# RWKV-7 attention fused with a cosine-gated feed-forward block: one scaling moved to VectorE, a product tree cut in three and moved, one step taken forward, three small products moved apart

## The chip, the cores and the metric

The kernel runs on one core of one Trainium2 chip. The metric is device time in microseconds (us) of one execution; the median of 3 runs of the kernel before is 802.15 us (800.43 to 803.71). The engines are named as in the profile: PE is TensorE's matmul, PEld its weight load, DVE VectorE, ACT ScalarE, POOL GpSimd, SP the engine whose queue issues nearly all DMAs here.

## The reference

For each of 4 batches and 8 heads a 40 x 40 state is carried over 768 tokens; the result feeds a feed-forward block with 2048 hidden units, whose weights arrive as float64.

```python
y[:, :, t] = einsum('bhd,bhde->bhe', rt, state)
Sa = einsum('bhde,bhe->bhd', state, at)
state = state * wt[:, :, None, :] - einsum('bhd,bhe->bhde', Sa, bt) \
        + einsum('bhd,bhe->bhde', vt, kt)
...
x = y.transpose(0, 2, 1, 3).reshape(B * S, H * D)   # 3072 x 320
h = x @ w_in                                        # 320 x 2048
out = (h * cos(h)) @ w_out                          # 2048 x 320
```

## The kernel before

The recurrence is done in chunks of C = 32 tokens, 24 chunks in all, all batches and heads at once. A chunk c has five steps in its chain, which `main(c)` returns (L922): t (`ch_t`, L650: transposes of the state qz into s), q (`ch_q`, L661: qps from s and rT), x (`ch_x`, L676: x0ps from the triangle ag, vvm, aT and qz; copied out by ACT L696 and DVE L697), s (`ch_s`, L700: sps from the inverse rt and x0; DVE L719 makes sm), z (`ch_z`, L726: dps from kn, vvm, bn and sm; DVE L755 and L762 read it, POOL L756 scales the state by the chunk's decay, and L767 scales the output tile yt by wx). Two steps after z, `tokens` (L772) writes yt to a DRAM tile xd, and one step later reads it back transposed as xT, all in SP's queue, which runs in order.

Beside the chain, `p2(c+1)` (L914) prepares the next chunk in steps v, k and g: transposes (L605, L614) and the Gram matrices `gram` (L619), which DVE L637, ACT L642 and DVE L643 copy out. `p1(c)` prepares two chunks' decays and the triangular systems (pw, pa, pb, pn). The inverse rt of four chunks' systems is built at DVE; for chunks 0 to 7 it is done in two blocks, and the off-diagonal block is made on PE: `pair_first` (F1 to F7, L546) and `pair_second` (S1 to S7, L560), each 64 small matmuls into a tile `below`, S ending with an addition into rt on DVE (L567). Chunk n's step s needs Sn.

The running products of the decays of chunks 4 to 23 are taken for four chunks at once: `ws_fetch(q)` (L159, 640 KB) loads them, `ws_scan(q)` (L166) multiplies them in nine DVE instructions, five up a tree (L170) and four down (L175), and `ws_store(q)` (L178) writes them to DRAM, from where `load` reads them. q = 2 stands for chunks 8 to 11.

The feed-forward block is cut in pieces over pairs of chunks: `first_a` and `first_b` (the hidden layer `ph`, 256 tokens by 512 units), then two `second` (into `po`). `first_b` computes the 64-row tail of w_in first if the step before it was marked `small` (L820), else last. Weights are turned from float64 to float32 in the first 140 us by `rounded` (L224): per tile a DMA `words`, DVE L245, L246, L255, L261, ACT L249, L251, L258 and POOL L264. These go into a list `w_steps`.

The order is written out by hand. For every chunk there is a list `segs` of steps, with M where a piece goes. `step` (L346) issues a step's instructions, then whatever `later(n, ...)` had put n steps ahead, then some instructions off the lists of the inverse and of the weights: in chunk 2 two of `w_steps` per step (none after an F or S), in chunk 3 two and three. Engines run what they are issued in order, so this list is the order of every engine. `FILL` (L1049) puts idle bf16 matmuls into PE's stream ahead of some places; `busy` (L955) puts idle 128x512 ones after a step:

```python
step(seg, *((0, 0) if c < 3 and seg in (*firsts, *seconds) else fill), small=seg in (...))
if seg not in (*firsts, *seconds) and (c < 2 or c == 2 and not done):
    busy({s: 6, q: 5, v: 4, k: 4, z: 4}.get(seg, 3))
```

`done` counts the pieces issued so far; it is 0 until chunk 2's first M. PSUM tiles named `at` (L324: sT, vT, qps, kT, x0ps, gram, sps, below, dps, wT, aps, bT, nps) share a ring of two buffers, so each waits until the tile two before it has been read.

Of the kernel before, what the change touches and what calls it, by code (L numbers as in the profile page):

```python
# [12 lines left out]
ALU = mybir.AluOpType  # L13
# [7 lines left out]
def kernel(  # L21
# [43 lines left out]
    nc = tc.nc  # L65
    B, H, S, D = r.shape
    P, C, DP = 128, 32, 64
# [95 lines left out]
            bass.AP(w.tensor, w.offset + q * n, [[S * D, B * H], [C * D, 4], [1, C * D]]),  # L163
        )

    def ws_scan(q):  # L166
        n = 1
        while n < C:
            to = ws[:, 2 * n - 1 :: 2 * n]
            nc.vector.tensor_tensor(to, to, ws[:, n - 1 :: 2 * n], ALU.mult)  # L170
            n *= 2
        n = C // 4
        while n:
            to = ws[:, 3 * n - 1 :: 2 * n]
            nc.vector.tensor_tensor(to, to, ws[:, 2 * n - 1 : C - 1 : 2 * n], ALU.mult)  # L175
            n //= 2

    def ws_store(q):  # L178
        wd[q] = dram.tile([B, H, 4, C, D], F32, tag="wd", name="wd")
# [166 lines left out]
    def step(work, of_inv=0, of_w=0, small=False):  # L346


        before = list(waiting)
        work()  # L350
        G["small"] = small and G["kind"]
        for w in before:
            w[0] -= 1
            if w[0] == 0:
                waiting.remove(w)
                w[1]()
        for steps, n in ((inv_steps, of_inv), (w_steps, of_w)):
            for _ in range(min(n, len(steps))):
                steps.pop(0)()
# [366 lines left out]
    def ch_z(c):  # L726
        ps = [at("dps") for _ in range(2)]
        sm = G["sm"]

        wide = c > 3  # L730
        for bb in range(0 if wide else B):
            for e in range(2):
                mm(
                    ps[bb // 2][full[e], bb % 2, : 4 * N72], idle[blk[bb], :DP],
                    pick(idle[blk[bb]], 0, (0, 4), (1, N72)), True,
                )
        for s, n in ((0, kn_b[c % 2]), (1, bn_b[c % 7])):
            for j in range(4):
                o = C - C * (j // 2)
                for bb in range(B):  # L740
                    for e in range(2):
                        first = wide and not s
                        mm(
                            ps[bb // 2][(full if first else half)[e], bb % 2, j * N72 : (j + 1) * N72],
                            n[blk[bb], 2 * j + e, : DP if first else D],
                            sm[e][blk[bb], j, :] if s else vvm[c % 2][blk[bb], 2 * j + e, o : o + N72],
                            first and j == 0,
                        )
        wx, wc = G["wx", c], G["wc", c]
        yt = sb1.tile([P, 4, B, C], F32, tag="yt", name="yt")  # L750
        for bb in range(B):
            dp = ps[bb // 2][:, bb % 2]
            if c < NCH - 1:
                z = pick(qz[:, bb], C, (DP, 2), (NZ, 2), (1, D))
                nc.vector.tensor_tensor(z, pick(dp, 0, (2 * N72 + C, 2), (N72, 2), (1, D)), z, ALU.add)  # L755
                nc.gpsimd.tensor_tensor(  # L756
                    z, z,
                    wc.rearrange("p (f m b) -> p f m b", f=2, m=2)[:, :, :, bb]
                    .unsqueeze(3).to_broadcast([P, 2, 2, D]),
                    ALU.mult,  # L760
                )
            nc.vector.tensor_tensor(  # L762
                yt.rearrange("p (f m) b t -> p f m b t", f=2)[:, :, :, bb],
                pick(dp, D, (2 * N72 - D, 2), (N72, 2), (1, C)),
                pick(qz[:, bb], 0, (NZ - C, 2), (NZ, 2), (1, C)), ALU.add,
            )
        nc.gpsimd.tensor_tensor(  # L767
            yt.rearrange("p j b t -> p (j b) t"), yt.rearrange("p j b t -> p (j b) t"), wx, ALU.mult
        )
        later(2, lambda: tokens(c, yt))  # L770
# [133 lines left out]

        return [first_w, both_a, lambda: p1_b(c), lambda: p1_n(c)]

    def scanned(q):

        ws_scan(q)
        later(2, lambda: ws_store(q))  # L910
        if q + 1 < NCH // 4:
            later(12, lambda: ws_fetch(q + 1))
# [17 lines left out]
    with tc.manual_schedule():  # L930
# [71 lines left out]
        v, k, g = p2(0)  # L1002
# [43 lines left out]
        firsts = [lambda n=n: pair_first(0, n, n > 2) for n in range(4)]  # L1046
        seconds = [lambda n=n: pair_second(0, n, n > 2) for n in range(4)]
        (F1, F2, F3), (S1, S2, S3) = firsts[1:], seconds[1:]
        FILL = {(1, 6): 6, (1, 9): 14, (2, 0): 6, (2, 3): 6, (2, 5): 4, (2, 11): 29, (3, 3): 13, (3, 4): 20}  # L1049
        for c in range(NCH):  # L1050
            t, q, x, s, z = main(c)
            v, k, g = p2(c + 1) if c + 1 < NCH else [lambda: None] * 3
# [2 lines left out]
            if c == 0:  # L1055
                segs = []
            elif c == 1:
                segs, fill = [t, F1, v, q, k, S1, x, g, s, z], (1, 4)
            elif c == 2:
                for n, m, name in ((11, 5, "a"), (14, 4, "b")):  # L1060
                    later(n, lambda m=m, name=name: load(m, name))
                segs, fill = [t, F2, v, q, S2, k, M, x, M, F3, g, M, s, S3, M, z, M, M], (0, 2)
            elif c == 3:
                pw4, pa4, pb4, pn4 = p1(4)
                pw, pa, pb, pn = p1(6)
                segs = [
                    t, pw4, M, q, pa4, M, x, lambda: scanned(2), M, s, pw, M, pb4, pa, M, pn4, M, z, M,
                    pb, v, pn, k, M, g,
                ]
                for n, m, name in ((1, 5, "b"),):  # L1070
                    later(n, lambda m=m, name=name: load(m, name))
                fill = (2, 3)
            elif c == 4:
                pw, pa, *p8 = p1(8)
                firsts = [lambda n=n: pair_first(4, n) for n in range(4)]
                seconds = [lambda n=n: pair_second(4, n) for n in range(4)]
                F4, F5, F6, F7 = firsts
                S4, S5, S6, S7 = seconds
                segs = [
                    t, v, M, q, M, k, x, M, F4, M, S4, F5, M, s, F6, M, pw, F7, M, z, M, g, M, pa, S5, lambda: scanned(3),  # L1080
                ]
                fill = (2, 0)
            elif c == 5:
                pw, pa = p1(10)[:2]
                pb, pn = p8
                segs = [t, M, pb, q, M, pn, k, M, x, M, s, S6, M, z, M, S7, M, pw, v, M, g, pa, M]
            elif c % 4 == 0 and q0 < NCH:
                pb, pn = p1(q0)[2:]
                segs = [t, v, M, q, M, k, x, M, g, M, s, pb, M, z, M, pn, M, M]
                if q0 + 4 < NCH:  # L1090
                    segs.insert(-1, lambda: scanned(c // 4 + 2))
            elif c % 4 == 1 and q0 < NCH:
                pw, pa = p1(q0 + 2)[:2]
                segs = [t, M, pw, q, M, x, k, M, s, v, M, z, M, pa, M, g, M, M]
            elif c % 4 == 2 and q0 < NCH:
                pb, pn = p1(q0 + 2)[2:]
                segs = [t, M, pb, q, M, pn, v, M, x, M, s, k, M, g, M, z, M, M]
            elif c % 4 == 3 and q0 + 4 < NCH:
                pw, pa = p1(q0 + 4)[:2]
                segs = [t, M, pw, q, M, x, k, M, s, v, M, z, M, pa, M, g, M, M]  # L1100
            else:
                segs = [t, v, M, q, M, x, k, M, g, M, s, M, M, z, M, M]
# [10 lines left out]
            for i, seg in enumerate(segs):  # L1113
                kept_busy(FILL.get((c, i), 0))
                while seg is s and ("rt", c) not in G:
                    if allowed(c):
                        piece(4, 0)
                    else:
                        inv_steps.pop(0)()
                while seg is pn4 and w_steps:  # L1120
                    w_steps.pop(0)()
                if seg is not M:
                    G["kind"] = "q" if seg is q and c > 3 else "other"
                    step(seg, *((0, 0) if c < 3 and seg in (*firsts, *seconds) else fill), small=seg in (q, x, g, s, z, pn, pn4, *firsts, *seconds))
                    if seg not in (*firsts, *seconds) and (c < 2 or c == 2 and not done):
                        busy({s: 6, q: 5, v: 4, k: 4, z: 4}.get(seg, 3))
                else:
                    place += 1
                    if place * empty // places > (place - 1) * empty // places:
                        continue  # L1130
                    if allowed(c) and (c != 4 or done < 23):
                        piece(*fill)
                while i == n - 1 and c > 3 and done < goal and c != 4 and allowed(c):
                    piece(*fill)
                if seg is pn and (c == 3 or c > 4 and c % 4 == 2):
                    inv_steps.extend(by_blocks(q0) if c == 3 else inverse(q0))
# [36 lines left out]
```

## Time and profile before

| what | value |
|---|---|
| median of 3 runs | 802.15 us (800.43 to 803.71) |
| the profiled execution: its own time | 800.58 us |
| its span (first to last instruction) | 798.9 us |
| PE busy in the span | 745.9 us (93%) |
| PE busy, 0 to 100 us | 68.98 of 100 us |
| PE busy, 100 to 260 us | 148.65 of 160 us |
| PE busy, 260 to 740 us | 474.96 of 480 us |
| DVE busy, 60 to 100 us / 100 to 120 / 120 to 160 | 36.06 of 40 / 11.70 of 20 / 33.59 of 40 us |

The profile is one execution, taken by the hardware profiler. Its first lines give each engine's busy time. Its timeline gives, per group of like instructions, the start, the length from the first start to the last end, the engine, the line, what is written and read, the shape, the count, and in brackets the engine's idle time just before it with what ended that. "issue" there means that the engine waited for nothing that the profile shows. The view by windows gives busy time and number of instructions of each engine in a stretch, and then the clock that TensorE was granted there as a share of full speed, the DMA engines' busy share and GB/s. Chunk 2 runs from about 93 to 129 us, chunk 3 to 170, chunk 4 to 206, chunk 5 to 242.

### The profile page before, as it was taken

What the parts mean: (1) busy time and instruction counts of PE and PEld (TensorE: products, weight loads), DVE (VectorE), ACT (ScalarE), POOL (GpSimd) and SP (SyncE); (2) the same over time, 40 slices, a digit from 0 to 9 for tenths busy, and PEclk for the clock granted to TensorE, in tenths of its full rate; (3) what the DMA queues carried; (4) which work ended last, traced back from release to release, by engine and by line L of the source; (5) the groups of instructions that cost most, each with busy time, mean ns of one, the idle gap of its engine ahead of it and who ended that gap; (6) DMA issues with size and microseconds to landing.
All of it is one profiled execution on the core that took longest, in us unless ns stands there. A gap on an engine that the chain in (4) does not pass through costs nothing.

```text
span 798.9 us, 39602 instructions
## 1 busy us (share of the span) xinstructions
PE 745.9 (93%) x17812; PEld 571.0 (71%) x17812; DVE 486.7 (61%) x1025; ACT 383.4 (48%) x723; POOL 199.9 (25%) x354
## 2 busy tenths in 40 slices
PE   4768798999999999999999999999999999999997
PEld 4535576777766777777777787777787777777775
DVE  8768858864734896554895645994346863323331
ACT  1336567564435436545535635534545445354352
POOL 5326635230321330330330230332031122201000
PEclk9888899999999999999999999999999999999999
DMA  8575563343353314334214324223220222001000
GB/s 112 150 187 140 146 152 88 60 124 64 59 122 64 67 36 65 72 99 70 60 38 66 93 43 73 46 49 68 43 46 21 46 46 55 19 18 32 20 17 16
DMA packets 183304, 55.79 MB, mean 70 GB/s; under 512 B 157152, under 2 KB 178656, under 8 KB 183136
## 3 DMA queue, kind: packets, MB, share of 16 engines
q1 hardware_dynamic: 177440, 52.11, 30.6%
q8 instruction: 140, 2.29, 1.2%
q10 hardware_dynamic: 5440, 0.82, 0.8%
q0 software_dynamic: 256, 0.33, 0.3%
q14 instruction: 28, 0.23, 0.1%
HBM read 42.07 MB, written 11.14 MB: 67 GB/s over the span
## 4 chain that ended last, share of the span: by engine, by line
PE 65%; DVE 14%; DMA 5%; ACT 5%; issue 4%; POOL 3%; SPq 2%; DVEq 0%; ACTq 0%; POOLq 0%
PE ph L101 22%; PE po L101 20%; PE x0ps L101 3%; PE dps L101 3%; PE gram L101 3%; DVE rw L395 3%; PE vT L330 2%; PE sps L101 2%; PE qps L101 2%; PE nps L101 2%; DVE inv_tmp L494 2%; DVE inv L498 2%; DVE mant L245 1%; SPq L152 1%; PE kT L330 1%
## 5 line engine op out<-in xcount | busy, mean ns | idle before, releaser
L101 PE MATMUL po<-w_out_sb,gT 128*128 128x320 f32 x768 | 223.5, 439 | 0.1
L101 PE MATMUL ph<-xT,w_in_sb 128*128 128x256 f32 x768 | 185.7, 386 | 0.1
L101 PEld LDWEIGHTS po<-w_out_sb,gT 128*128 128x128 f32 x768 | 140.2, 190 | 54.6 <-issue 2.3
L101 PEld LDWEIGHTS ph<-xT,w_in_sb 128*128 128x128 f32 x768 | 139.3, 190 | 29.7 <-issue 12.4
L830 ACT ACTIVATE turns<-ph,rnd 128x512 f32<-128x512 f32 x96 | 64.1, 685 | 156.3 <-PE ph L101 155.9
L832 DVE SCALAR_TENSOR_TENSOR turns<-turns,ph 128x512 f32<-128x512 f32 x96 | 64.0, 683 | 109.4 <-ACT turns L830 109.2
L840 DVE TENSOR_TENSOR gT<-ph,turns 128x512 f32<-128x512 f32 x96 | 65.8, 686 | 38.4 <-ACT turns L837 38.4
L756 POOL TENSOR_TENSOR qz<-qz,wc 128x160 f32<-128x160 f32 x92 | 41.9, 475 | 168.5 <-DVE qz L755 167.9
L837 ACT ACTIVATE turns<-turns,half_pi 128x512 f32<-128x512 f32 x96 | 69.3, 722 | 3.1
L836 ACT ACTIVATE turns<-turns 128x512 f32<-128x512 f32 x96 | 60.1, 626 | 19.0 <-DVE turns L832 19.0
L101 PE MATMUL ph<-xT,w_in_tail 64*128 64x256 f32 (+1 forms) x512 | 54.6, 394 | 1.6 <-issue 1.6
L498 DVE TENSOR_TENSOR inv<-inv,inv_tmp 128x31 f32<-128x31 f32 (+15 forms) x124 | 51.2, 413 | 4.3
L755 DVE TENSOR_TENSOR qz<-dps,qz 128x160 f32<-128x160 f32 x92 | 28.9, 314 | 37.6 <-PE dps L101 37.3
L586 POOL COPY vp<-nat_v 128x320 f32<-128x320 f32 x24 | 11.7, 487 | 159.9 <-DMA nat_v<-in_v_dram 139.6
L494 DVE TENSOR_TENSOR inv_tmp<-u,inv 128x31 f32<-128x31 f32 (+15 forms) x124 | 48.5, 391 | 2.3
L395 DVE RECIPROCAL rw<-nat_w 128x320 f32<-128x320 f32 x20 | 42.8, 2142 | 0.1
L101 PEld LDWEIGHTS ph<-xT,w_in_tail 64*128 64x128 f32 (+1 forms) x512 | 32.2, 160 | 10.8 <-issue 7.3
L767 POOL TENSOR_TENSOR yt<-yt,wb 128x512 f32<-128x512 f32 x24 | 31.6, 1318 | 22.1 <-DVE yt L762 22.1
L659 ACT COPY s<-sT 104x416 f32<-104x416 f32 x46 | 20.8, 503 | 33.1 <-PE sT L655 33.1
L719 DVE TENSOR_TENSOR sm<-sps,su 128x128 f32<-128x128 f32 x48 | 11.7, 285 | 33.1 <-ACT sm L714 30.3
L396 POOL TENSOR_TENSOR bn<-nat_b,rw 128x320 f32<-128x320 f32 x22 | 19.9, 905 | 44.3 <-DVE rw L395 44.2
L671 ACT COPY qz<-qps 40x512 f32<-40x512 f32 x46 | 26.6, 579 | 6.8 <-PE qps L101 6.4
(136 smaller groups left out, 1100.3 us busy)
## 6 DMA issues: line engine op xcount, KB each, us to landing
words<-in_moe_w_in_dram SPq DMA_DIRECT2D x8, 512.0 KB
xd<-yt SPq DMA_DIRECT2D x48, 80.0 KB
out_dram<-ot SPq DMA_DIRECT2D x24, 160.0 KB
nat_k<-in_k_dram SPq DMA_DIRECT2D x92, 40.0 KB
nat_v<-in_v_dram SPq DMA_DIRECT2D x92, 40.0 KB
nat_r<-in_r_dram SPq DMA_DIRECT2D x92, 40.0 KB
nat_a<-in_a_dram SPq DMA_DIRECT2D x84, 40.0 KB
ws<-in_w_dram SPq DMA_DIRECT2D x5, 640.0 KB
```

What stands on the lines that cost most here:

```text
L101: nc.tensor.matmul(o, lhsT=lhsT, rhs=rhs, start=start, stop=stop, skip_group_check=True)
L395: nc.vector.reciprocal(rw, wn)
L494: nc.vector.tensor_tensor(tmp, u[:, j : j + 1, :j].to_broadcast([P, C - j, j]), x[:, j:, j : j + 1].to_broadcast([P, C - j, j]), ALU.mult,)
L498: nc.vector.tensor_tensor(x[:, j:, :j], x[:, j:, :j], tmp, ALU.subtract)
L755: nc.vector.tensor_tensor(z, pick(dp, 0, (2 * N72 + C, 2), (N72, 2), (1, D)), z, ALU.add)
L756: nc.gpsimd.tensor_tensor(z, z, wc.rearrange("p (f m b) -> p f m b", f=2, m=2)[:, :, :, bb] .unsqueeze(3).to_broadcast([P, 2, 2, D]), ALU. ...
L767: nc.gpsimd.tensor_tensor(yt.rearrange("p j b t -> p (j b) t"), yt.rearrange("p j b t -> p (j b) t"), wx, ALU.mult)
L830: nc.scalar.activation(n, u, ACTF.Identity, bias=rnd, scale=1.0)
L832: nc.vector.scalar_tensor_tensor(n, n, -ROUND, u, ALU.add, ALU.subtract)
L836: nc.scalar.activation(n, n, ACTF.Abs)
L837: nc.scalar.activation(n, n, ACTF.Sin, bias=half_pi, scale=-2.0 * math.pi)
L840: nc.vector.tensor_tensor(gT[:, 2 * e : 2 * e + 2].rearrange("p f t -> p (f t)"), us[e], ns[e], ALU.mult)
```

## The change

1. In chunks 1 and 3, yt is scaled by VectorE instead of GpSimd.
2. `ws_scan` takes a range of its nine instructions. The scan of q = 2 stood in chunk 3 as one step after x; now it stands in chunk 2 as three steps of three instructions, after the first M, after g and after s. These steps take nothing off `w_steps`. The store follows two steps, the next fetch twelve steps after the third.
3. In chunk 2, x stands ahead of the first M instead of behind it. The M that follows a scan step is no longer preceded by a `small` step. The entry of FILL moves with its place, the third M.
4. S3 moves from behind s to behind z and one M. S6 moves from behind s to behind z and one M, S7 from ahead of pw to behind pw.
5. Step g for chunk 4 moves from the end of chunk 3 to chunk 4, behind t, with an M between it and v.

```diff
-    def ws_scan(q):
-        n = 1
+    def ws_scan(lo=0, hi=9):
+        work, n = [], 1
         while n < C:
-            to = ws[:, 2 * n - 1 :: 2 * n]
-            nc.vector.tensor_tensor(to, to, ws[:, n - 1 :: 2 * n], ALU.mult)
+            work.append((ws[:, 2 * n - 1 :: 2 * n], ws[:, n - 1 :: 2 * n]))
...
+        for to, by in work[lo:hi]:
+            nc.vector.tensor_tensor(to, to, by, ALU.mult)
...
-        nc.gpsimd.tensor_tensor(
+        (nc.vector if c in (1, 3) else nc.gpsimd).tensor_tensor(
             yt.rearrange("p j b t -> p (j b) t"), yt.rearrange("p j b t -> p (j b) t"), wx, ALU.mult
         )
...
-    def scanned(q):
-        ws_scan(q)
+    def scanned(q, lo=0, hi=9):
+        ws_scan(lo, hi)
+        if hi < 9:
+            return
         later(2, lambda: ws_store(q))
...
-        FILL = {..., (2, 5): 4, (2, 11): 29, (3, 3): 13, (3, 4): 20}
+        FILL = {..., (2, 5): 4, (2, 13): 29, (3, 3): 13, (3, 4): 20}
...  c == 2
-                segs, fill = [t, F2, v, q, S2, k, M, x, M, F3, g, M, s, S3, M, z, M, M], (0, 2)
+                scan = [lambda n=n: scanned(2, n, n + 3) for n in (0, 3, 6)]
+                segs, fill = [t, F2, v, q, S2, k, x, M, scan[0], M, F3, g, scan[1], M, s, scan[2], M, z, M, S3, M], (0, 2)
...  c == 3
-                    t, pw4, M, q, pa4, M, x, lambda: scanned(2), M, s, pw, M, pb4, pa, M, pn4, M, z, M,
-                    pb, v, pn, k, M, g,
+                    t, pw4, M, q, pa4, M, x, M, s, pw, M, pb4, pa, M, pn4, M, z, M,
+                    pb, v, pn, k, M,
                 ]
+                g4 = g
...  c == 4
-                    t, v, M, q, M, k, x, M, F4, M, S4, F5, M, s, F6, M, pw, F7, M, z, M, g, M, pa, S5, lambda: scanned(3),
+                    t, g4, M, v, q, M, k, x, M, F4, M, S4, F5, M, s, F6, M, pw, F7, M, z, M, g, M, pa, S5, lambda: scanned(3),
...  c == 5
-                segs = [t, M, pb, q, M, pn, k, M, x, M, s, S6, M, z, M, S7, M, pw, v, M, g, pa, M]
+                segs = [t, M, pb, q, M, pn, k, M, x, M, s, M, z, M, S6, M, pw, S7, v, M, g, pa, M]
...
-                    step(seg, *((0, 0) if c < 3 and seg in (*firsts, *seconds) else fill), small=...)
+                    step(seg, *((0, 0) if c < 3 and seg in (*firsts, *seconds, *scan) else fill), small=...)
```

More of the change, by code (lines that the diff above doesn't have):

```diff
@@ L173, in ws_scan @@
         while n:
-            to = ws[:, 3 * n - 1 :: 2 * n]
-            nc.vector.tensor_tensor(to, to, ws[:, 2 * n - 1 : C - 1 : 2 * n], ALU.mult)
+            work.append((ws[:, 3 * n - 1 :: 2 * n], ws[:, 2 * n - 1 : C - 1 : 2 * n]))
             n //= 2
+        for to, by in work[lo:hi]:
+            nc.vector.tensor_tensor(to, to, by, ALU.mult)
     def ws_store(q):
@@ L1048 @@
         (F1, F2, F3), (S1, S2, S3) = firsts[1:], seconds[1:]
-        FILL = {(1, 6): 6, (1, 9): 14, (2, 0): 6, (2, 3): 6, (2, 5): 4, (2, 11): 29, (3, 3): 13, (3, 4): 20}
+        FILL = {(1, 6): 6, (1, 9): 14, (2, 0): 6, (2, 3): 6, (2, 5): 4, (2, 13): 29, (3, 3): 13, (3, 4): 20}
+        scan = []
         for c in range(NCH):
@@ L1123 @@
                     G["kind"] = "q" if seg is q and c > 3 else "other"
-                    step(seg, *((0, 0) if c < 3 and seg in (*firsts, *seconds) else fill), small=seg in (q, x, g, s, z, pn, pn4, *firsts, *seconds))
+                    step(seg, *((0, 0) if c < 3 and seg in (*firsts, *seconds, *scan) else fill), small=seg in (q, x, g, s, z, pn, pn4, *firsts, *seconds))
                     if seg not in (*firsts, *seconds) and (c < 2 or c == 2 and not done):
```

## The prediction

> **What bounds the kernel now.** First the busy times, then the stretches of 20 us.
>
> ```profile
> PE 745.9 (93%) x17812; PEld 571.0 (71%) x17812; DVE 486.7 (61%) x1025; ACT 383.4 (48%) x723; POOL 199.9 (25%) x354
> ...
> q8 instruction: 140, 2.29, 1.2%
> ```
>
> PE bounds it: from 100 to 740 us it is busy for 97% of the time. The second line is PE's own program: 2.29 MB over its 35624 instructions (17812 twice) is 64 bytes each, so one of the 140 packets holds 256 instructions, or 128 matmuls with their weight loads.
>
> An edit in chunks 1 to 5 (93 to 242 us) is thus worth what it takes from PE's gaps or adds to PE's work. Third, the waits of PE from 90 to 290 us:
>
> ```profile
> PE dps L101 <- issue: 1.9, 2, 1.6
> PE ph L101 <- issue: 1.6, 1, 1.6
> ...
> PE dps L101 <- DVE rt L567: 0.7, 1, 0.7
> ...
> PE aps L330 <- ACT wb L378: 0.7, 1, 0.7
> PE vT L330 <- DVE vvm L643: 0.6, 1, 0.6
> ...
> PE aps L330 <- DVE sm L719: 0.4, 1, 0.4
> ```
>
> The list adds up to some 12 us, and the diff touches about 5.6: 1.57 and 1.61 us of "issue", 0.72 of dps behind S3's addition, 0.62 of vT behind gram's copies, 0.36 of aps behind sm, 0.67 of aps behind ACT. That is the room for a gain.
>
> Fourth, what "issue" is. By the view by windows PE had started 2633 matmuls when it stopped at 122.5 us and 5297 at 228 us; at the stops that end at 59.83, 74.78 and 78.50 us 976, 1358 and 1486. The distances, 382, 128, 1147 and 2664, are 3, 1, 9 and 21 times 128 within the few records that are missing. PE stops at the same place of a 256-instruction packet each time: it has run out of program. Both late stops follow on dense runs of small matmuls: s, S3, z (64, 64, 136), and s, S6, z (64, 64, 128). There a packet lasts under 2 us.
>
> Last, the timeline of chunk 2:
>
> ```profile
> 101.58 1.03 PE L101 MATMUL busy<-idle 128*128 128x512 bf16 x4
> ...
> 110.46 1.28 DVE L832 SCALAR_TENSOR_TENSOR turns<-turns,ph 128x512 f32<-128x512 f32 x2 [1.39 <-ACT turns L830]
> ...
> 120.73 0.28 DVE L567 TENSOR_TENSOR rt<-rt,below 128x128 f32<-128x128 f32 x1
> ...
> 122.13 1.28 DVE L832 SCALAR_TENSOR_TENSOR turns<-turns,ph 128x512 f32<-128x512 f32 x2 [1.12 <-ACT turns L830]
> ...
> 124.11 0.36 PE L101 MATMUL dps<-sm,bn 32*40 32x72 f32 x14 [1.57 <-issue]
> ```
>
> DVE has holes of 1.39 and 1.12 us here, but it turns weights between them without a rest.
>
> **The change, part by part.** *yt on VectorE.* POOL loses 1.46 us (chunk 1, 94.11) and 1.28 us (chunk 3); DVE gains 0.68 each, by a gT product of the same shape. In chunk 1 DVE has 2.86 us idle ahead of 106.42 to hide it, and its L261 beside POOL's scaling took 1.76 us instead of 0.69, so up to 1.07 comes back. xd leaves at 95.59 now; SP is free at 94.11, so at most 1.48 us earlier, and the xT, nat_k and words behind it in SP's queue with it. PE is idle for 0.08 us between 100 and 120, so none of it pays there: 0. In chunk 3 the 0.68 stands ahead of gT products that po reads at 166, over 2 us later: 0; uncovered it would cost 0.68.
>
> *x first.* x now comes while no piece is done, so the list puts `busy(3)` behind it: three idle matmuls at 1.03/4 us, **+0.77** on a full PE. The first_b's put their tails last: 1.82 + 1.07 us by the rows at 137.99 and 139.81, where chunk 2's take 2.98 and 3.34 now: -0.1 and -0.45.
>
> *The scan.* Its nine instructions took 3.79 us at 146: thirds of 1.63, 0.63 and 1.53. Its data were fetched at 55.5, so it waits for no DMA. The first third falls into the hole of 1.39 (longer if the words land earlier). The second stands ahead of a weight step on which ACT L258, then L714, then sm hang: sm 0.6 later. The third stands ahead of L832 and z's L755: the 1.12 and 0.54 us of holes and S3's 0.28 make up for it. Uncovered, the whole costs 3.79. The store leaves SP after the last words (124.9), while SP waits for yt; the next fetch (0.60 us of SP, 640 KB) comes 23 us earlier, amid chunk 3's loads, of which the last (nat_r, 162.7) is needed by PE at 171: 0. In chunk 3, aps no longer waits behind the scan: **-0.36**.
>
> *S3.* dps loses the wait of 0.72, and 64 matmuls go out of the dense run, so the place where the program ran out moves 61 matmuls on: 14 left of z, 8 of po and into S3. The packet that came at 121.9 to 122.9 is then needed later than z: -1.57 for z, if PE is not held otherwise. But S3's tile now follows dps in the ring, so S3 waits for z's L755 and L762, which stand behind the third scan part; and wT of chunk 3 waits for S3's addition, which DVE does behind L840, L245 to L261 and L255 of the weights: L255 ends at 130.94 in the rows of before, so with z's part some 0.4 later the addition ends near 131.6, and PE could start wT at 129.5. Behind wT on PE stand first_a, 13 and 20 idle matmuls, q and aps. From both sides, up to aps (137 us): all gone, 0.77 - 0.55 - 0.72 - 1.57 = -2.1, and -3.2 if both ACT waits of chunk 3 (0.45, 0.67) shrink with it; everything new felt, +1.9. I take **+0.3**: DVE, not PE, sets the pace to 137 us, it gets 3.8 us more to do, and its holes come to 3.05 (1.39, 1.12, 0.54).
>
> *g of chunk 4.* vT's tile follows gram's by one; with t ahead and an M of 1.9 us between g and v its wait is covered: **-0.62**. p2_in(5) comes a step later and still stands in POOL's queue well ahead of vT.
>
> *S6, S7.* The place of the second stop moves into S6, 64 matmuls on, or 1.2 us by the rows (fb's remainder and S6), so 0.3 of 1.61 stays: -1.3; a gap of 0.33 inside dps that hangs on S6 goes too. S7 between wT and vT makes vT wait for wT's copies (L378, 1.07 us behind wT; S7 fills 0.66): +0.5. Sum **-1.1**, bounds -1.9 and +0.7.
>
> Sum: 0.3 - 0.36 - 0.62 - 1.1 = -1.8 us. Against the profiled execution's 800.58 us (span 798.9 and 1.7 around it) that is 798.8; the median of the runs, 802.15, lies 1.6 above it, so I forecast 802.15 - 1.8 = 800.35, rounded to **800.4 us**.
>
> The Trainium skill, page "Runtime: NRT & Kernel Launch", section "Instruction fetch mechanics", says that a program streams in blocks of 256 instructions and that fetching is hidden, since dispatch is slower than the refill. The block agrees with the 64 bytes above; the hiding does not, with stops of 1.57 and 1.61 us at equal places of a block. By the page the stops would be something else, the gains counted on them, 0.8 and 1.3, would fall away, and the sum would be +0.3.
>
> **The rivals.** *All covers hold.* DVE hides the scan, S3's addition is early: -3.2 - 0.36 - 0.62 - 1.9 = -6.1, or 796.1 us. For it: the holes, and POOL off DVE's back; against it: DVE is busy for 17.4 of 20 us from 120 on.
>
> *The stops stay, elsewhere.* The change doesn't set the dense runs apart where it counts: PE runs dry in another run of small matmuls, as it did five times before 80 us. The +0.3 above counts on about half of the first stop, 0.8, and chunk 5 on 1.3: -1.8 + 0.8 + 1.3 = +0.3, or 802.5 us. Against: the places move past z in both chunks.
>
> *The clock drops* (the other side). The granted clock fell after gaps no longer than 1.54 us:
>
> ```profile
> 74.99:78.40 3.41, 1.98 (x128) 1.21 (x109) 2.89 (x5) 2.49 (x4) 1.54 (x1) 1.00 0.56 108
> 78.40:81.81 3.41, 3.31 (x97) 1.74 (x98) 2.43 (x4) 1.62 (x4) 1.23 (x1) 0.50 0.64 156
> ...
> 122.77:126.18 3.41, 2.07 (x21) 1.50 (x21) 2.87 (x11) 3.21 (x5) 1.22 (x3) 1.00 0.30 82
> 126.18:129.60 3.42, 3.42 (x20) 2.57 (x19) 3.42 (x6) 1.02 (x2) 2.12 (x4) 1.00 0.36 121
> ```
>
> The number after the POOL column is the granted clock. 1.98 us of PE work in 3.41 were followed by half speed, 2.07 were not, and 122.8 to 126.2 is the spot where S3 is to wait. One more wait of 0.1 us there decides. Price: 1.7 us for each such stretch of 3.41 us, two (S3's wait, wT's wait), on top of +1.9 for the waits and with chunks 3 to 5 giving 1.0 only: 1.9 + 3.4 - 1.0 = +4.3, or 806.5 us.
>
> The Trainium skill, page "TensorE: Matmul & The Clock Gate", section "HAM oscillation — how this bites in real kernels", asks only that PE have no idle gap above about 3.4 us; by it this rival would cost nothing, while the rows above show half speed behind a gap of 1.54.
>
> **How the numbers follow.** The forecast with its own range 798.4 to 802.4: 0.48. All covers hold: 0.20, counted as faster by over 0.5% (4.0 us, about what a measurement of this kernel can tell from no change). Stops stay: 0.20. Clock: 0.12, counted as slower. So faster 0.20, same 0.68, slower 0.12. The range leaves out the outer halves of the first and last rival: 796.5 to 805.5.
>
> **What would show it.** After: no "issue" gap above 1 us in z of chunk 2 or first_b of chunk 5; dps without a wait on rt; three idle matmuls more at 104; wT of chunk 3 near 131 with a wait on DVE rt L567; vT of chunk 4 without a wait, vT of chunk 5 with one on ACT wb; clock 1.00 throughout from 92 us. Wrong would make it: a new dense run, a DVE backlog that passes 140 us, or half speed behind 120.

## The result, and the profile after

| | before | after |
|---|---|---|
| median, 20 runs each | 802.30 us (799.39 to 804.73) | 804.07 us (801.07 to 808.48) |
| ratio | 1 | 1.0031, 95% interval 1.0018 to 1.0045 |
| profiled execution: its time, its span | 800.58, 798.9 us | 805.99, 804.2 us |
| chunk 2 (first sT to first sT) | 35.83 us | 39.57 us |
| chunks 3 and 4 | 77.14 us | 77.00 us |
| chunk 5, chunk 6 | 35.99, 30.51 us | 33.97, 31.36 us |

The changed kernel is 2.5 us (1.4 to 3.6) slower. The time lies inside the range, the sign is the other one. The two profiled executions lie 5.4 us apart, 1.7 below and 1.9 above their medians; 1.45 us of that had come by the start of chunk 1, where the program is the same. So the chunk lengths of one pair show where to look, and the timed comparisons below decide.

First the busy times and the program's own queue, after:

```profile
PE 748.7 (93%) x17815; PEld 571.7 (71%) x17815; DVE 490.5 (61%) x1027; ACT 383.5 (48%) x723; POOL 197.4 (25%) x352
...
q8 instruction: 140, 2.29, 1.2%
```

Three matmuls more (the idle ones behind x), 2.8 us more of busy PE, 3.8 more of VectorE. Next the waits of PE from 90 to 290 us (total, times, longest):

```profile
PE dps L101 <- DVE sm L719: 3.7, 2, 2.2
PE busy L101 <- issue: 1.7, 1, 1.7
PE wT L330 <- DVE rt L567: 1.4, 1, 1.4
PE po L101 <- issue: 1.4, 1, 1.4
PE aps L330 <- DMA nat_a<-in_a_dram: 1.3, 1, 1.3
PE ph L101 <- DVE gT L840: 0.9, 1, 0.9
```

Against the list of before, the two stops of 1.6 us in dps and ph, the wait on rt ahead of dps and the 0.7 on ACT are gone, as forecast. In their place stand waits that the list of before did not have. Of the 3.7 us on sm, 1.5 stand at the end of chunk 1, where the kernel before waits 3.3 us (until 88.43, just before the list starts); the 2.2 in chunk 2 are new, and the largest. The stop of 1.7 us in busy stands ahead of chunk 2's first sT (94.00); e3 and e4, whose code up to there is that of before, have it too (1.45 us each). The timeline of chunk 2 after, all engines, in order of time, shows what is behind it:

```profile
111.07 2.54 DVE L176 TENSOR_TENSOR ws<-ws 128x640 f32<-128x640 f32 x3
111.23 1.68 POOL L264 TENSOR_TENSOR w_out_sb<-w_out_sb,sign 128x512 f32<-128x512 f32 x1 [5.63 <-DVE w_out_sb L261]
...
116.50 1.97 PE L101 MATMUL ph<-xT,w_in_sb 128*128 128x256 f32 x8 [0.92 <-DVE gT L840]
...
120.18 1.83 DVE L176 TENSOR_TENSOR ws<-ws 128x80 f32<-128x80 f32 x3
120.41 1.15 POOL L264 TENSOR_TENSOR w_out_sb<-w_out_sb,sign 128x512 f32<-128x512 f32 x1 [7.30 <-ACT expo L249]
...
121.93 0.96 DVE L255 SCALAR_TENSOR_TENSOR mant<-words,mant 128x512 f32<-128x512 uint32 x1
...
124.05 0.49 DVE L719 TENSOR_TENSOR sm<-sps,su 128x128 f32<-128x128 f32 x2 [1.16 <-ACT sm L714]
...
124.68 0.45 PE L101 MATMUL dps<-idle 32*64 32x288 bf16 x4 [2.17 <-DVE sm L719]
...
125.72 2.51 DVE L176 TENSOR_TENSOR ws<-ws 128x120 f32<-128x120 f32 x3
125.95 1.15 POOL L264 TENSOR_TENSOR w_out_sb<-w_out_sb,sign 128x512 f32<-128x512 f32 x1 [3.61 <-ACT expo L249]
...
127.01 4.42 PE L101 MATMUL po<-w_out_sb,gT 128*128 128x320 f32 x8
...
136.58 0.66 PE L330 MATMUL wT<-ident,nat_w 128*128 128x128 f32 x4 [1.43 <-DVE rt L567]
```

Before, the nine instructions stood in chunk 3, where GpSimd multiplied nothing:

```profile
145.93 2.21 DVE L170 TENSOR_TENSOR ws<-ws 128x640 f32<-128x640 f32 x5
148.05 1.82 DVE L175 TENSOR_TENSOR ws<-ws 128x40 f32<-128x40 f32 x4
```

Read the timeline after in pairs: each third of the scan (L176) starts within 0.3 us of one of GpSimd's multiplications of weights by their sign (L264), and takes 2.54, 1.83 and 2.51 us, not 1.63, 0.63 and 1.53. Behind the second third stand L255, ACT's L258 and L714, then sm, and dps waits 2.17 us. The eight po matmuls behind it take 4.42 us; later ones in the same chunk take 2.42. The view by windows, cut at the edges where the clock changes, says why (PE's busy time is the first number behind the length, the granted clock the number behind POOL):

```profile
120.85:124.26 3.41, 1.67 (x14) 0.80 (x12) 2.25 (x5) 1.22 (x4) 1.50 (x3) 1.00 0.66 179
124.26:127.67 3.41, 2.99 (x133) 2.67 (x134) 3.34 (x8) 2.43 (x4) 1.15 (x1) 0.50 0.50 146
127.67:131.09 3.42, 3.42 (x8) 2.02 (x6) 3.42 (x10) 2.20 (x4) 0.75 (x2) 0.50 0.48 193
```

A stretch with 1.67 us of PE work in 3.41 is followed by two stretches at half clock. The amount of work alone doesn't decide that: in f4 a stretch with 1.66 us of work in 3.41 (127.68 to 131.09) is followed by full clock.

### The profile page after: what moved, and what is told of

Its sections match the earlier page's. It is cut to its first block, busy times and chain, and to the rows that moved or that the text cites. A ratio compares the mean times of both kernels' runs of the same rounds, so it can differ in the third digit from the quotient of the medians.

```text
span 804.2 us, 39605 instructions
## 1 busy us (share of the span) xinstructions
PE 748.7 (93%) x17815; PEld 571.7 (71%) x17815; DVE 490.5 (61%) x1027; ACT 383.5 (48%) x723; POOL 197.4 (25%) x352
## 4 chain that ended last, share of the span: by engine, by line
PE 67%; DVE 13%; DMA 5%; ACT 4%; issue 4%; POOL 3%; SPq 3%; DVEq 0%; POOLq 0%; ACTq 0%
PE ph L101 23%; PE po L101 20%; PE x0ps L101 4%; PE dps L101 3%; PE gram L101 3%; PE vT L330 2%; DVE rw L395 2%; SPq L152 2%; PE sps L101 2%; PE qps L101 2%; DVE inv_tmp L494 2%; DVE inv L498 2%; PE nps L101 2%; PE kT L330 1%; DVE turns L832 1%
## 5 line engine op out<-in xcount | busy, mean ns | idle before, releaser
L767 POOL TENSOR_TENSOR yt<-yt,wb 128x512 f32<-128x512 f32 x22 | 28.9, 1312 | 22.1 <-DVE yt L762 22.1
L101 PEld LDWEIGHTS <-idle 128*128 128x128 bf16 (+2 forms) x271 | 18.1, 99 | 17.2 <-issue 11.7
```

The source lines that it names most:

```text
L101: nc.tensor.matmul(o, lhsT=lhsT, rhs=rhs, start=start, stop=stop, skip_group_check=True)
L767: (nc.vector if c in (1, 3) else nc.gpsimd).tensor_tensor(yt.rearrange("p j b t -> p (j b) t"), yt.rearrange("p j b t -> p (j b) t"), wx, ...
```

## The experiments

Theory D: what costs is the place of the scan, on VectorE ahead of the steps that sm hangs on and beside GpSimd. Rival S: it is S3's late addition. Later rivals are named where they come up. Every ratio is to the kernel before on the same chip, with its 95% interval; the us are the ratio times some 799.

| kernel | parts | ratio | us |
|---|---|---|---|
| after | all | 1.0031 (1.0018 to 1.0045) | +2.5 |
| e1 | scan in thirds | 1.0020 (1.0003 to 1.0036) | +1.6 |
| e2 | all but the scan | 1.0032 (1.0013 to 1.0051) | +2.6 |
| e3 | g of chunk 4, S6, S7 | 0.9986 (0.9962 to 1.0010) | -1.1 |
| e4 | S3 | 0.9991 (0.9973 to 1.0009) | -0.7 |
| e5 | yt, x first | 1.0029 (1.0003 to 1.0055) | +2.3 |
| e6 | S3, S6, S7 | 0.9980 (0.9956 to 1.0003) | -1.6 |
| e7 | all, less three L264 | 0.9983 (0.9964 to 1.0002) | -1.4 |
| e8 | S6, S7 | 0.9998 (0.9972 to 1.0025) | -0.2 |
| f1 | x first | 1.0013 (0.9991 to 1.0035) | +1.0 |
| f2 | yt of chunks 1 and 3 | 1.0009 (0.9986 to 1.0032) | +0.7 |
| f3 | scan behind k, S3, g, S6, S7 | 0.9978 (0.9960 to 0.9997) | -1.8 |
| f4 | all, scan in one step behind x | 0.9994 (0.9973 to 1.0016) | -0.5 |
| g1 | x first, no idle matmuls | 1.0005 (0.9982 to 1.0028) | +0.4 |
| g2 | yt of chunk 1 | 1.0032 (1.0009 to 1.0054) | +2.6 |
| g3 | scan ahead of x, S3, g, S6, S7 | 0.9978 (0.9958 to 0.9998) | -1.8 |
| g4 | scan ahead of x, g, S6, S7 | 0.9967 (0.9943 to 0.9990) | -2.6 |

Most of these effects are below 0.3%, so only the larger ones stand alone. e1, e3, e4 and e5 hold all of the change between them and give 1.6 - 1.1 - 0.7 + 2.3 = +2.1, against +2.5 for the whole; but their intervals together make that sum uncertain by some 3.4 us either way, so it is no strong test.

**The scan alone (e1).**

```diff
-  segs = [t, F2, v, q, S2, k, M, x, M, F3, g, M, s, S3, M, z, M, M]
+  segs = [t, F2, v, q, S2, k, M, x, scan[0], M, F3, g, scan[1], M, s, S3, scan[2], M, z, M, M]
```

> The kernel before with the scan of chunks 8 to 11 alone moved into chunk 2 as three steps (x, S3, g, S6, S7 and yt as before). Theory D (the scan's second third stands on VectorE ahead of the weight steps that sm hangs on, and each third is slowed beside GpSimd's scaling of weights: 6.9 us in the changed kernel's profile for 3.8 in the profile of before): the dps of chunk 2 waits 1.5 us or more on VectorE, PE falls below 2 us busy in a stretch of 3.41 us, half clock follows; chunk 2 is 3 to 4 us longer, chunk 3 about 0.5 shorter, the whole 2.5 to 4 us slower. Rival S (S3's late addition is what costs in chunk 2): the scan alone is hidden or costs under 1 us, with the dps of chunk 2 waiting under 1 us for sm. Rival N (the difference is noise and the place in the 3.41 us grid): within 1 us of before.

The sign is theory D's, the size is less: +1.6 us. In its profile the thirds take 2.54, 1.83 and 2.42 us, dps waits 1.89 us for sm and 1.06 more for rt, the clock falls to 0.63 and 0.68 from 120 to 130 us, and chunk 2 lasts 39.51 us. dps waits more than rival S allowed, so the scan is not hidden; its time alone (0.2 to 2.9 us) would not tell.

**Everything but the scan (e2).**

```diff
-  segs, fill = [..., k, x, M, scan[0], M, F3, g, scan[1], M, s, scan[2], M, z, M, S3, M], (0, 2)
+  segs, fill = [..., k, x, M, M, F3, g, M, s, M, z, M, S3, M], (0, 2)
```

> The changed kernel with the scan put back into chunk 3 as one step; all its other parts stay. Theory D: the loss in chunk 2 goes with the scan, the gains of chunks 4 and 5 stay: 1 to 3 us faster than before, the clock 1.00 behind 100 us, dps of chunk 2 without a wait on rt. Rival S: S3's addition still comes late and wT of chunk 3 waits over 1 us for it: within 1 us of before or slower. Rival N: within 1 us of before.

A miss: +2.6 us. Chunk 2 is indeed short again, 35.50 us, without a wait on sm. In its profile the loss is in chunk 4, 41.96 us long: its first M waits 3.48 us. The profile names DVE's inv L525, which has no part in it; the transfers read xT, issued at 169.67 and 170.11, and the M starts at 171.88. With the scan in chunk 3, its store and the next fetch, 640 KB each, go out at 160.80 and 164.34, right ahead of xd at 165.02; and g, moved out from ahead of that M, no longer covers the wait for xT. How much of the 2.6 us is this wait isn't shown: e3 has a wait like it and is no slower than before, and e2 also holds yt and x, which cost 2.3 together (e5, below).

**Chunks 4 and 5 (e3), and S6, S7 alone (e8).**

```diff
-                    pb, v, pn, k, M, g,
+                    pb, v, pn, k, M,
...
-                    t, v, M, q, M, k, x, M, F4, M, S4, ...
+                    t, g4, M, v, q, M, k, x, M, F4, M, S4, ...
...
-                segs = [t, M, pb, q, M, pn, k, M, x, M, s, S6, M, z, M, S7, M, pw, v, M, g, pa, M]
+                segs = [t, M, pb, q, M, pn, k, M, x, M, s, M, z, M, S6, M, pw, S7, v, M, g, pa, M]
```

> The kernel before with g of chunk 4 behind t of chunk 4 and S6, S7 set apart; nothing of chunks 1 to 3 is changed but that g leaves the end of chunk 3. Theory D: vT of chunk 4 no longer waits (0.6 us), the program stop of 1.6 us and the gap of 0.3 in chunk 5 go, vT of chunk 5 waits about 0.5 us; the stop comes again in chunk 6 in part: 0.5 to 2 us faster. Rival M (the stop only moves, each dense run has its stop): within 0.5 us of before.

> The kernel before with S6 and S7 alone set apart in chunk 5. By the prediction's steps 1.1 us faster (a stop of 1.6 us in part and a gap of 0.3 gone, a wait of 0.5 new). Since the kernel with g of chunk 4 moved as well came out only 1.1 us faster, in two groups of times, with a wait of 2.1 us for xT in chunk 4: if g's move is what spoils it, this one is 1 to 2.5 us faster, in one group. Rival M (the stop goes to chunk 6 in whole): within 0.5 us of before.

e3 comes to -1.1 us, with times from 794.1 to 802.2, and its profile shows the same collision as e2's:

```profile
171.07 2.12 SPq L788 DMA_DIRECT2D xT<-xd  x2
...
173.58 3.37 PE L101 MATMUL ph<-xT,w_in_sb 128*128 128x256 f32 x8 [2.08 <-DMA xT<-xd]
```

So g's move meets this wait where the scan's transfers stay in chunk 3: the kernels with both moved (after, e7, f3, f4, g3, g4) have chunk 4 at 35.97 to 36.57 us and no such wait. Whether g's move by itself gains anything there, no run shows. e8, without g, gives -0.2 us, where a gain of 1 to 2.5 was expected: nearer to rival M, though the interval (-2.2 to +2.0) leaves both open. The stop in chunk 5 does go, and chunk 5 takes 33.97 to 34.58 us in the ten kernels with S6 and S7 apart, 34.34 to 35.99 in the eight without (medians 34.03 and 34.68): 0.65, not 1.1. The stop of 1.61 in the profile of before was a long one; others at the same place took 0.95 to 1.31, and e4 had none above 0.8. And in three of the ten profiles a stop came in chunk 6 (after 1.39, f3 1.67, e7 0.84).

**S3 alone (e4), and with S6, S7 (e6).**

```diff
-  segs = [..., s, S3, M, z, M, M]
+  segs = [..., s, M, z, M, S3, M]
```

> The kernel before with S3 alone moved behind z and one M in chunk 2. Theory D: dps loses its wait on rt (0.7 us) and the program stop of 1.6 us in z; wT of chunk 3 waits about 0.5 us for S3's addition, since VectorE has no scan in chunk 2: chunk 2 is 1.5 to 2.3 us shorter, the whole 0.5 to 2 us faster. Rival S: wT of chunk 3 waits over 1 us for S3's addition, S3 itself waits for z's readers, and half clock follows: within 0.5 us of before or up to 2 us slower.

> The kernel before with S3 behind z and one M, and S6 and S7 set apart; the scan, g, x and yt as before. If the two gains add: chunk 2 is 1 to 4 us shorter than in the other runs with S3 ahead of z, minus 1.7 for wT's wait on S3's addition and the half clock behind it; chunk 5 1 to 2 us shorter: 1 to 2.5 us faster than before. Rival M (the stops of PE's program only move): within 0.7 us of before.

e4 gives -0.7 us (-2.2 to +0.7), e6 -1.6 (-3.5 to +0.2). In e4 the wait on rt ahead of dps and the stop inside z's second part are gone; a stop of 0.98 stands in its first part, wT waits 1.75 us for S3's addition, and half clock follows. The gain is traded for a new wait, as rival S said, though at no loss. e6's interval leaves both its readings open.

**GpSimd's three multiplications left out (e7).**

```diff
-            nc.gpsimd.tensor_tensor(dst, dst, t["sign"], ALU.mult)
+            if m not in (13, 14, 15):
+                nc.gpsimd.tensor_tensor(dst, dst, t["sign"], ALU.mult)
```

> The changed kernel without GpSimd's scaling by the sign for the three weight tiles beside which the scan's thirds ran (its output is not the reference's there); nothing else is changed. Theory D: the scan's thirds go back from 2.54, 1.83 and 2.51 us to 1.6, 0.6 and 1.5, sm comes 1.2 us earlier or more, dps of chunk 2 waits under 1.2 us instead of 2.2: 1 to 3 us faster than the changed kernel, so within 1 us of before. Rival B (VectorE is simply too full, beside GpSimd or not): under 0.7 us faster than the changed kernel.

The run that decides. -1.4 us against before, so 3.8 us (2.0 to 5.7, from the two ratios and their intervals) below the changed kernel, for three instructions of 1.16 us on an engine that is busy for a quarter of the time. Its timeline, all engines (line numbers from 265 on are one higher):

```profile
106.04 1.70 DVE L176 TENSOR_TENSOR ws<-ws 128x640 f32<-128x640 f32 x3
...
114.70 0.58 DVE L176 TENSOR_TENSOR ws<-ws 128x80 f32<-128x80 f32 x3
...
117.81 0.33 PE L101 MATMUL dps<-idle 32*64 32x288 bf16 x8
...
118.72 1.58 DVE L176 TENSOR_TENSOR ws<-ws 128x120 f32<-128x120 f32 x3
...
128.64 1.09 PE L331 MATMUL wT<-ident,nat_w 128*128 128x128 f32 x8 [1.75 <-DVE rt L568]
```

The thirds are back at 1.70, 0.58 and 1.58 us, dps starts without a wait, the clock stays at 1.00, chunk 2 takes 35.57 us. wT's wait for S3's addition is there as in the changed kernel, 1.75 against 1.43: it isn't what cost. A rival is that the kernel gains by the missing multiplications as such. The next run, f4, speaks against it: it keeps all three.

**The scan in another place (f3, f4).** Both put it in one step: f3 between k and the first M, with x and yt as before; f4 is the changed kernel with the scan behind x.

```diff
-  scan = [lambda n=n: scanned(2, n, n + 3) for n in (0, 3, 6)]
+  scan = [lambda: scanned(2)]
-  segs, fill = [..., k, x, M, scan[0], M, F3, g, scan[1], M, s, scan[2], M, z, M, S3, M], (0, 2)
+  segs, fill = [..., k, x, scan[0], M, M, F3, g, M, s, M, z, M, S3, M], (0, 2)        # f4
+  segs, fill = [..., k, scan[0], M, x, M, F3, g, M, s, M, z, M, S3, M], (0, 2)        # f3
```

> The kernel before with the scan of chunks 8 to 11 as one step between k and the first M of chunk 2, where VectorE has a hole of 2.9 us ahead of x's copy, S3 behind z and one M, g of chunk 4 behind its t, S6 and S7 set apart; x and yt as before. Theory D (what cost was the place of the scan, ahead of the steps that sm hangs on and beside GpSimd): the scan takes 3.8 to 5 us there without a new wait of PE, chunk 2 is no longer than before, dps of chunk 2 without a wait on sm; with the gains of g, S3, S6 and S7 the whole is 2 to 4 us faster than before. Rival B (VectorE is too full in chunk 2 at any place): within 1 us of before or slower.

> The changed kernel with the scan as one step behind x of chunk 2 (instead of three steps); all else as changed. Theory D: the nine instructions take about 3.8 us, done before GpSimd's next scaling; dps of chunk 2 without a wait on sm; about 3 to 4 us faster than the changed kernel, so 0 to 1.5 us faster than before, as the kernel without GpSimd's three scalings was. Rival B: 0 to 1 us faster than the changed kernel.

f4: -0.5 us against before, 3.0 (0.9 to 5.0) below the changed kernel, with every other part of the change in it. Its timeline:

```profile
104.35 3.95 DVE L176 TENSOR_TENSOR ws<-ws 128x640 f32<-128x640 f32 x9
...
109.65 1.16 POOL L264 TENSOR_TENSOR w_out_sb<-w_out_sb,sign 128x512 f32<-128x512 f32 x1 [7.24 <-DVE w_out_sb L261]
...
125.55 0.71 PE L101 MATMUL below<-rt,bn 32*32 32x16 f32 x64 [1.50 <-DVE yt L762]
...
131.08 1.09 PE L330 MATMUL wT<-ident,nat_w 128*128 128x128 f32 x8 [1.75 <-DVE rt L567]
```

All nine instructions take 3.95 us, over before the next multiplication. The three multiplications now run at 109.65, 117.85 and 121.47, largely in holes of VectorE, which waits for ACT until 110.97, 119.47 and 122.65: as such they cost it next to nothing. f3 is the first that is faster than before with an interval that excludes 1: -1.8 us, less than the 2 to 4 hoped for. Its scan starts beside the multiplication of w_in_tail and takes 4.78; ph then waits 1.48 us for gT, and the step brings three idle matmuls. So VectorE has room in chunk 2, but not for nothing.

**x first and yt (e5, f1, g1, f2, g2).**

```diff
-  segs = [..., k, M, x, M, F3, ...]
+  segs = [..., k, x, M, M, F3, ...]
...
-  if seg not in (*firsts, *seconds) and (c < 2 or c == 2 and not done):
+  if seg not in (*firsts, *seconds) and (c < 2 or c == 2 and not done and seg is not x):    # g1 alone
...
-        nc.gpsimd.tensor_tensor(
+        (nc.vector if c in (1, 3) else nc.gpsimd).tensor_tensor(    # g2: c == 1
```

> The kernel before with two parts alone: yt of chunks 1 and 3 scaled by VectorE, and x of chunk 2 ahead of the first M (which brings three idle matmuls). By the prediction's steps: 0.77 - 0.1 - 0.45 = +0.2 us, within 0.5 us of before. Rival P (the parts that looked free are what costs, since the kernel with all parts but the scan was as slow as the one with all): 1.5 us or more slower, through an earlier xd that meets other transfers or a stop of PE's program moved by the idle matmuls.

> The kernel before with x of chunk 2 ahead of the first M alone (and the three idle matmuls that this brings). The two parts x and yt together took 2.3 us (0.2 to 4.4). If x is what costs: 1.5 to 3 us slower than before. By the prediction's steps +0.2: within 0.7 us of before.

> The kernel before with x of chunk 2 ahead of the first M, and without the three idle matmuls that the list puts behind it. If the idle matmuls are what x costs (0.8 us): within 0.5 us of before, 1 us faster than with them. If the order itself costs (x's copy earlier, program stops at other places): 0.5 to 2 us slower, as with them.

> The kernel before with yt of chunks 1 and 3 scaled by VectorE alone. If yt is what costs (0.68 us ahead of VectorE's weight work in chunk 1, or xd and words at other times on the queues): 1.5 to 3 us slower than before. By the prediction's steps 0: within 0.7 us of before.

> The kernel before with yt of chunk 1 alone scaled by VectorE (chunk 3's by GpSimd, as before). If the 0.68 us ahead of VectorE's weight work in chunk 1 is what yt costs: 0.5 to 1.5 us slower than before. If it is chunk 3's, or nothing at all: within 0.4 us of before.

Together they cost 2.3 us (0.2 to 4.4), which the prediction had at +0.2. x first costs 1.0, without the idle matmuls 0.4: in keeping with the 0.8 of the idle matmuls, though the intervals don't part them. yt of chunk 1 alone costs 2.6 (0.7 to 4.3), with chunk 3's 0.7 (-1.1 to 2.6); the two agree only between 0.7 and 2.6, so the size is not settled. What yt's move does can be seen in the waits of SP's own queue from 86 to 101 us, before:

```profile
SPq L237 <- DVE mant L255: 3.9, 2, 3.3
SPq L786 <- DMA xd<-yt: 1.5, 1, 1.5
SPq L776 <- POOL yt L767: 1.5, 1, 1.5
```

and after:

```profile
SPq L237 <- DVE mant L255: 6.5, 3, 3.3
SPq L786 <- DMA xd<-yt: 2.7, 1, 2.7
```

The 1.5 us that xd waited for GpSimd are gone, as intended. But SP has `words` (L237) ahead of xd, and these wait for a buffer that VectorE's L255 frees; L255 now stands behind yt. xd leaves just behind the `words`, its landing takes longer (2.7 us of waiting instead of 1.5), and xT goes out 5.67 us after the start of chunk 2 instead of 4.89. g2 shows the same: `words` at 91.99, xd at 93.12, xT at 96.72, 5.35 us into the chunk. What PE loses by it isn't shown: in neither profile does PE wait for xT in chunk 2. In g2's the loss is in half clock from 92.1 to 99.0 us, behind a stop of 2.00 us ("issue") at 90.66, a place where kernels without yt's move stop for 1.2 to 1.5 us too (f3, e3, e4, g1).

**What is best (g3, g4).** The scan between the first M and x, so behind L255 and without more idle matmuls; S3 moved (g3) or not (g4).

```diff
+  segs = [t, F2, v, q, S2, k, M, scan[0], x, M, F3, g, M, s, M, z, M, S3, M]      # g3
+  segs = [t, F2, v, q, S2, k, M, scan[0], x, M, F3, g, M, s, S3, M, z, M, M]      # g4
```

> The kernel before with the scan as one step between the first M and x of chunk 2 (so behind L255 of the weights instead of ahead of it, and without three more idle matmuls), S3 behind z and one M, g of chunk 4 behind t, S6 and S7 set apart; x and yt as before. Theory D: the scan fills VectorE's hole ahead of x's copy, the wait of 1.5 us that ph had for gT shrinks by 1 us, the idle matmuls' 0.75 are gone: 2.5 to 4.5 us faster than before. Rival B (VectorE's chain up to z's readers is what sets chunk 2's end, any scan ahead of it costs): 0.5 to 2 us faster, as the kernel with the scan behind k was.

> The same kernel with S3 left behind s, ahead of z, as before. If S3's move gains what it seemed to (0.7 us alone): 0.5 to 1.5 us slower than with it. If the stop that it removes only uncovers the wait of S3 for z's readers and of wT for S3's addition: within 0.5 us of the kernel with it, or faster.

g4, with S3 where it was, is the best of all: -2.6 us against before (-4.6 to -0.8), some 5 below the changed kernel. g3's -1.8 is not told apart from it; it falls short of the 2.5 to 4.5 expected and into rival B's range. The two profiles show the trade: g4 has stops of 1.40 and 1.54 us in first_b and z, g3 none of these but 1.49 ahead of S3 (on yt L762) and 1.75 ahead of wT (on rt L567).

## Why the prediction was wrong

- **The scan: the step that failed.** "Its nine instructions took 3.79 us at 146: thirds of 1.63, 0.63 and 1.53" took the durations from a place where GpSimd multiplied nothing. In chunk 2 they took 6.88. The chain was named rightly ("on which ACT L258, then L714, then sm hang: sm 0.6 later"), but sm came 1.83 later by the third alone, and 0.28 more by L255, which took 0.96 instead of 0.68 beside GpSimd's copies. dps waited 2.17, and half clock followed. The whole is 3.8 us (2.0 to 5.7) by e7; the scan alone, in the kernel before, cost 1.6 (0.2 to 2.9, e1). The prediction had +0.3 for all of chunks 2 and 3. The same text had read the sign of it in the trace of before: L261 took 1.76 us instead of 0.69 beside GpSimd's scaling. It counted that as a gain and did not ask what runs beside the scan.
- **The Trainium skill** has the rule, page "SBUF — State Buffer", section "Who interferes with whom": a VectorE instruction with two SBUF inputs and a GpSimd instruction that reads SBUF exclude each other, and the one that comes later waits until the first is done. The runs agree: the second instruction of the first third took 1.33 us beside L264 and 0.49 without it in f4, those of the other two 1.17 and 1.38 where they take 0.20 and 0.45, and L264 itself 1.68 instead of 1.16 where the scan was first. By the page each third could have been priced with one such multiplication more, 3 x 1.16 = 3.5 us as an estimate; 3.0 was measured (6.88 against 3.86 in e7).
- **"The clock drops", 0.12**, was the right rival with the wrong trigger. Two stretches at half clock came at 124.3, behind 1.67 us of work in 3.41; but behind the wait on sm, not on S3 or wT. Its rule, that the border lies between 1.98 and 2.07 us of PE work in a stretch of 3.41, fitted the rows of before and not the later runs: 1.66 us was followed by full clock (f4 at 127.68, g3 at 126.77), and 2.15 and 2.19 by half (g3 at 72.14, g4 at 72.99). What decides stays open. That the time fell inside the range is owed to this rival's price, not to its cause.
- **In chunk 3, aps, -0.36.** The wait behind sm went, but aps then waited for the load of nat_a: 1.33 us in the changed kernel, 0.96 in e1, 1.47 in e7, 0.7 and 0.8 in f3 and f4, none in g3 and g4. Chunk 3 lasts 40.92 us against 40.85, though g has left it. The prediction took the loads of chunk 3 as free of cost; why this one is late in some kernels stays open.
- **yt on VectorE, "0"**, was wrong by 2.6 us (0.7 to 4.3) by g2; f2, with chunk 3's, gives 0.7 and doesn't exclude 0. "At most 1.48 us earlier" looked at xd alone; ahead of it in SP's queue are `words`, and they hang on the engine that got the work. Into the chunk, xd left 0.5 us earlier (2.11 against 2.61) and xT 0.8 later; how PE loses time by it isn't shown.
- **x first, +0.77**: the three idle matmuls took 0.82 at 105.87. That the time is theirs fits f1 and g1 (1.0 and 0.4) without being shown by them.
- **S3.** The wait of 0.72 and the stop of 1.57 went, as stated, and wT of chunk 3 does wait for S3's addition (1.43 in the changed kernel, 1.75 in e4 and f4). The balance is about nothing (e4 -0.7, g3 against g4 +0.8): the stop lay beside VectorE's work up to L762, and without it S3 waits 1.5 us there.
- **g of chunk 4, -0.62**: the wait went, vT of chunk 4 starts without one in the changed kernel. What was not seen is that it needs the scan out of chunk 3: without that it meets xT (3.48 in e2, 2.08 in e3).
- **S6, S7, -1.1**: the new wait came as forecast (0.56 on wb at 239.34, by POOL's L391 instead of ACT's copy), the stop went, but it was worth less than one profile showed and came again in chunk 6 in 3 of 10.

Open: how much yt costs and by what path, whether x's order costs anything beyond its idle matmuls, and why a stop at one place of the program takes 0.95 us in one execution and 1.61 in another. Not tried: the scan's parts between L255 and sm, where VectorE waits 1.16 us for ACT.

## What to carry to other kernels

Price a moved instruction by what runs beside it at its new place, on the engine that it shares data paths with, not by its row at the old one. When work moves to another engine, look at what ahead in the same DMA queue hangs on the engine that takes it over: here `words`, ahead of xd. And a gain counted on one long stop in one profile should be checked against a second profile of the same code: here chunk 2 of e3, whose code up to the end of chunk 3 is that of before, took 40.08 us against 35.83.

## What the hardware showed

- Two-input products on VectorE and GpSimd in SBUF take turns: 0.20 became 1.17 us, 0.49 became 1.33, 0.45 became 1.38 on VectorE beside a 1.15 us product of GpSimd; GpSimd's 1.16 became 1.68 when VectorE's 0.82 us instruction was first. An instruction with one input can be held too: L245 took 1.33 us instead of 0.42 beside GpSimd's L767 (kernel before, 126.88).
- Half clock came behind 1.67 us of PE work in a stretch of 3.41 us (changed kernel), and in g2 behind 1.40 of 3.40 (88.6 to 92.0 us), both times for two stretches (0.50 and 0.50; 0.52 and 0.50). It did not come behind 1.66 of 3.41 in f4 (127.68 to 131.09) and g3 (126.77 to 130.18).
- In the kernel before, the stops of 1.0 us and more that end at 59.83, 74.78, 78.50, 124.11 and 229.55 us end 1.2 to 1.6 us after a packet of the program's queue (q8) has landed (at 58.60, 73.33, 77.23, 122.89 and 227.99), which fits the prediction's reading that PE had run out of program.
